# New hand-written instruction orders for all five queues, and four more normalizations on ScalarE, in a fused attention and gated-MLP block

## The chip, the core and the metric

One core of one Trainium2 chip. The metric is the device time of one execution in microseconds (us). The engines that matter: TensorE (PE; its weight loads are shown apart as PEld), VectorE (DVE), ScalarE (ACT), GpSimd (POOL), and the SP queue, which computes nothing and only issues DMAs. ScalarE's queue issues DMAs too.

## The reference

Two branches share one normalized input and are added to it. `x` is 2048 tokens x 512, all in bf16.

```
xn = layernorm(x)
# A: attention over 8 keys, 2 apart, 32 heads of 16
q, k, v = split(xn @ wqkv)
logits[s, w] = q[s] . k[s - 2w] / 4           (w = 0..7, masked where s - 2w < 0)
A = (softmax(logits) weighted sum of v[s - 2w]) @ wo
# B: gated MLP that mixes tokens
z = gelu(xn @ w_in);  z1, z2 = halves of 896
g = w_sp @ layernorm(z2) + b_sp               (w_sp is 2048 x 2048)
B = (z1 * g) @ w_out
out = x + A + B
```

## The kernel before

The kernel is straight-line code without loops on the chip. A small planner in the file (`Plan`) collects tasks. Each has an engine, a name, and the buffers that it reads and writes, from which its dependencies follow. `plan.orders` holds five lists, one for TensorE, ScalarE, VectorE, GpSimd and SP, and each names every task of its queue. A list therefore is the order in which that queue runs; the planner's costs and due times decide nothing more. Every queue is strictly in order: a task that waits holds up all that stand behind it.

The stages, with the names of the tasks and the lines of the profile:

- **Setup and layernorm of x**, for 16 tiles of 128 tokens. `ldx0..15` load rows of x (L588). Per tile, VectorE takes statistics (`bnst`, L650, and `bnag`, L653), GpSimd raises the variance to the power -1/2 (`rstd`, L655), and VectorE normalizes (`norm`, L665). Tiles 0 to 3 are transposed by TensorE (`xTr`, evacuated by `xTe`), tiles 4 to 15 by DMA transposes from SP (`xTd`, L669). GpSimd also makes masks (`mask`, `hm`). Weights come in by `ldq`, `ldk`, `ldw_in1`, `ldwv`, `ldwout`, `ldwo` and others.
- **Q and K**, for four groups j of 512 tokens and four channel groups c: `Qj_c`, `Kj_c` (L733), evacuated together by ScalarE as `QKej_c` (L741); `halo` copies the last 16 columns for the next group (L747).
- **Logits**: VectorE multiplies Q by eight shifted K (`prodj_c`, 4096 columns, L757) and adds the four channel groups (`paddj_n`, L762). TensorE sums over the head with `lgj` (L772), ScalarE evacuates (`lge`).
- **z2 and its norm**: `z2_b` (L852), gelu with a sum by ScalarE (`z2g`), sum of squares (`z2s`, L907). Per wave j of four token tiles VectorE forms mean and variance (`zm`, `zq`, `ze`, `zv`), GpSimd the power -1/2 (`zr`, L926), VectorE a bias (`zb`), and then each tile b is normalized by `znb`, either on ScalarE (L933) or on VectorE (L937). `znact` says where, one entry per wave.
- **z1 and V**: `z1_b` (L895) with gelu `z1g` (L901), `Vq` (L717) with `Ve` (L721).
- **Softmax**: `pT` transposes logits by DMA, `sm`, `ssub`, `sexp` (ScalarE), `sz`, `srec`, `sattn`.
- **Gate and output**, eight steps t, each for two of the 16 output tiles, from tile 14 and 15 down to 0 and 1. The spatial product of 2 x 2 blocks is done with seven products instead of eight: `P1_t` to `P7_t` (L1015), which need sums of weights (`S13`, `S2`, `S4`; L974, L978, L980) and of z2 (`T1` to `T4`, L954). SP brings the weights by DMA transposes straight from DRAM, `wt_0` and `wt_1` (L962), into two slots. ScalarE copies partial results (`cA`, `cB`, `cE`, `g11`, `g21`), VectorE makes `g12` (L1057), `g22` (L1061) and the gated `u` (L1039), which SP transposes (`uT`, L1041). For attention VectorE multiplies (`pv`, L1145) and adds (`pva`, L1149; `pvc`, L1153), and SP transposes (`OTdt`, L1157). `outb` is the final product (L1207 for attention, L1211 for the MLP), onto x put into PSUM by `os`; `fin` evacuates, `st` stores. ScalarE's queue issues `ldxrt`, the rows of x for the residual (L1166), and most `st` (L1182).

PSUM banks are handed out in a fixed turn, so a product waits until ScalarE has emptied its bank. The lines that decide where a norm runs, and what waits for what around it:

```
 655  T("pool", lambda g: g.tensor_tensor(Fv("rstd", 1, b), Fv("mv", 1, 2 * b + 1), Fv("mhalf", 1), ALU.pow),
 656    reads=[("mv", b), "mhalf"], writes=[("rstd", b)], est=580, name="rstd%d" % b)
 ...
 665  T("dve", lambda v: v.tensor_scalar(AC(xo, [[1, 512]]), xin, Fv("mv", 1, 2 * b),
 666                                     Fv("rstd", 1, b), ALU.subtract, ALU.mult),
 ...
 932  if cfg["znact"][j]:
 933      T("act", (lambda b: lambda a: a.activation(A("z2", FH, FH * b), A("z2", FH, FH * b), ACTF.Identity,
 934                                                 bias=Fv("nb2", 1, b), scale=Fv("rstd2", 1, b)))(b),
 935        reads=[("nb2", j), ("rstd2", j)], writes=[("z2l", b), ("z2r", b)], est=c_act(FH), name="zn%d" % b)
 936      continue
```

Of the kernel before, what the change touches and what calls it, by code (L numbers as in the profile page):

```python
# [325 lines left out]
def build_kernel(nc, A_x, A_wqkv, A_wo, B_x, B_w_in, B_w_sp, B_b_sp, B_w_out, out, report=False, sched_kw=None,  # L326
# [90 lines left out]
    with ExitStack() as es:  # L417
# [809 lines left out]
        for t in range(NT):  # L1227
# [16 lines left out]
        plan.orders = [  # L1244
            """
                warm xTr0b fill0 xTr0a z2_0_0b z2_0_1b z2_0_0a xTr1a xTr1b z2_0_1a xNr z2_1_0a z2_1_0b z2_1_1a xTr2a
                xTr2b z2_1_1b z2_2_0a z2_2_0b xTr3b xTr3a z2_2_1a z2_2_1b z2_3_0a z2_3_1a z2_3_1b z2_3_0b Q0_0 K0_0
                Q0_1 Q0_2 K0_1 Q0_3 K0_2 K0_3 Q1_0 K1_0 K1_1 Q1_2 Q1_1 K1_2 Q1_3 K1_3 z2_4 z2_5 z2_6 z2_7 K2_0 Q2_0
                Q2_1 Q2_2 K2_1 K2_2 Q2_3 lg0_0 K2_3 z2_8 z2_9 z2_10 z2_11 K3_0 Q3_0 K3_1 K3_2 Q3_2 K3_3 Q3_3 Q3_1
                z2_13 lg1_0 z2_14 z2_12 z1_14 z1_15 z2_15 z1_13 z1_10 z1_12 z1_8 z1_11 lg2_0 z1_7 z1_9 z1_6 z1_2 z1_4  # L1250
                z1_5 z1_1 z1_3 z1_0 V10 V11 lg3_0 V14 V12 V15 V13 V8 V4 V6 V9 V5 V7 V2 V3 V0 V1 P1_0 P5_0 P6_0 P2_0
                bits P3_0 P7_0 P1_1 P5_1 P4_0 P6_1 P2_1 P7_1 P3_1 P1_2 P4_1 P2_2 P6_2 P5_2 P7_2 P3_2 out14_0 P4_2 P1_3
                out15_0 P2_3 P6_3 P5_3 P1_4 P7_3 P3_3 out12_0 P4_3 P5_4 P6_4 out13_0 P2_4 P7_4 P3_4 P1_5 P4_4 out10_0
                P2_5 P5_5 P6_5 out11_0 P7_5 P3_5 P5_6 P4_5 P1_6 out9_0 P6_6 out8_0 P2_6 out6_0 P1_7 P3_6 P7_6 out7_0
                P5_7 P6_7 P4_6 P2_7 P3_7 P7_7 out4_0 out5_0 P4_7 out3_0 out2_0 out0_0 out1_0 out1_1 out1_2
            """.split(),
            """
                actprime ldw_in2a_1 ldw_in2b_1 ldx2 ctr0 xTe0b xTe0a xTe1a xTe1b xNe z2g0_0 xTe2a xTe2b z2g0_1 z2g1_0
                xTe3a xTe3b z2g2_0 z2g2_1 z2g1_1 z2g3_0 z2g3_1 QKe0_0 z2s0 QKe0_1 QKe0_2 QKe0_3 z2s1 QKe1_0 z2s2
# [17 lines left out]
                prod0_2 bnag12 bnag15 bnst14 bnst13 padd0_1 bnag14 bnag13 prod0_3 norm12 padd0_2 norm15 norm13 norm14
                prod1_0 prod1_1 ze0 padd1_0 zm1 prod1_2 zv0 padd1_1 prod1_3 zq1 zb0 padd1_2 ze1 prod2_0 prod2_1 zm2
                padd2_0 zv1 prod2_2 padd2_1 zq2 prod2_3 padd2_2 zb1 zm3 prod3_0 prod3_1 ze3 zq3 padd3_0 smask ze2
                prod3_2 zv2 padd3_1 zv3 prod3_3 padd3_2 S13_0 zn15 zn8 zn12 zn9 T3_0 zn13 zn10 S2_0 zn14 S4_0 T3_3  # L1280
                zn11 T1_0 T1_3 T3_2 T2_0 sm1_3 T3_1 sm2_3 T2_3 sm3_3 T1_1 ssub3 T2_1 T1_2 T4_0 T4_3 T2_2 sz1_3 T4_1
# [72 lines left out]
```

## Time and profile before

| | |
|---|---|
| median of 3 runs | 231.41 us (230.76 to 232.58) |
| the profiled execution | 229.84 us, span of its instructions 228.1 us |
| granted TensorE clock | 1.000 |
| busy: TensorE, VectorE, ScalarE, GpSimd | 221.1, 211.7, 131.1, 30.7 us |
| moved by DMA | 29.96 MB, mean 131 GB/s |

Times in the views are us from the start of the span. A view of a timeline gives start, length, engine, line, operation, output and input, and in square brackets how long the engine sat idle just before and what ended that; neighbours that do the same are merged (x2 and more). TensorE's busy time is modelled: a matmul counts as busy while it is in the pipeline. A queue's name with a q (SPq, ACTq) means its issuing of DMAs.

### The profile page before, as it was taken

What the parts mean: (1) busy time and instruction counts of PE and PEld (TensorE: products, weight loads), DVE (VectorE), ACT (ScalarE), POOL (GpSimd) and SP (SyncE); (2) the same over time, 40 slices, a digit from 0 to 9 for tenths busy, and PEclk for the clock granted to TensorE, in tenths of its full rate; (3) what the DMA queues carried; (4) which work ended last, traced back from release to release, by engine and by line L of the source; (5) the groups of instructions that cost most, each with busy time, mean ns of one, the idle gap of its engine ahead of it and who ended that gap; (6) DMA issues with size and microseconds to landing.
All of it is one profiled execution on the core that took longest, in us unless ns stands there. A gap on an engine that the chain in (4) does not pass through costs nothing.

```text
span 228.1 us, 3127 instructions
## 1 busy us (share of the span) xinstructions
PE 221.1 (97%) x1163; PEld 121.5 (53%) x1176; DVE 211.7 (93%) x259; ACT 131.1 (57%) x237; POOL 30.7 (13%) x35
## 2 busy tenths in 40 slices
PE   8999999999999999999999999999999998999975
PEld 6545554554676775655454545544454543454434
DVE  4799999999999999999999999999999996999920
ACT  4777989879999899874242504028133226033332
POOL 3345455050220090000000000000000000000000
DMA  6998502390000008939988999939498198427742
GB/s 226 278 188 244 113 15 49 77 241 4 0 3 0 0 0 187 223 87 265 231 140 185 185 177 205 159 80 200 95 205 216 37 172 150 86 92 79 182 86 92
DMA packets 77400, 29.96 MB, mean 131 GB/s; under 512 B 68669, under 2 KB 75339, under 8 KB 77259
## 3 DMA queue, kind: packets, MB, share of 16 engines
q1 hardware_dynamic: 74250, 25.08, 54.6%
q10 hardware_dynamic: 3136, 4.69, 6.8%
q8 instruction: 9, 0.15, 0.3%
q14 instruction: 5, 0.04, 0.1%
HBM read 9.05 MB, written 2.10 MB: 49 GB/s over the span
## 4 chain that ended last, share of the span: by engine, by line
PE 73%; DVE 13%; DMA 9%; issue 3%; ACT 1%; POOL 1%; SPq 0%; DVEq 0%
PE ps L1015 27%; PE ps L733 12%; PE ps L895 11%; PE ps L852 8%; PE ps L717 6%; PE ps L1211 5%; DMA arena<-in_B_w_sp_dram 4%; DVE arena L1149 3%; DVE arena L1145 3%; PE ps L1207 3%; DMA arena<-in_A_wqkv_dram 2%; DMA arena<-arena 1%; DMA arena<-in_A_x_dram 1%; DVE arena L974 1%; PE ps L772 1%
## 5 line engine op out<-in xcount | busy, mean ns | idle before, releaser
L1015 PE MATMUL ps<-arena 128*128 128x448 f16 (+1 forms) x448 | 87.2, 353 | 1.0 <-DVE arena L980 0.9
L1015 PEld LDWEIGHTS ps<-arena 128*128 128x128 f16 (+1 forms) x448 | 43.5, 98 | 43.1 <-DVE arena L980 1.3
L1030 ACT ACTIVATE ps<-ps 128x448 f32<-128x448 f32 x16 | 8.5, 530 | 49.9 <-DVE arena L1057 26.2
L757 DVE TENSOR_TENSOR arena<-arena 128x4096 bf16<-128x4096 bf16 x16 | 36.4, 2287 | 0.2
L1145 DVE TENSOR_TENSOR arena<-arena 128x4096 bf16<-128x4096 bf16 x16 | 36.1, 2278 | 0.0
L733 PE MATMUL ps<-arena 128*128 128x512 bf16 x124 | 28.0, 379 | 0.6 <-DMA arena<-in_A_wqkv_dram 0.4
L1149 DVE TENSOR_TENSOR arena<-arena 128x4096 bf16<-128x4096 bf16 (+1 forms) x16 | 28.0, 1749 | 0.0
L762 DVE TENSOR_TENSOR arena<-arena 128x4096 bf16<-128x4096 bf16 x12 | 27.4, 2287 | 0.1
L1211 PE MATMUL ps<-arena 128*128 128x512 bf16 (+2 forms) x125 | 27.1, 355 | 0.1
L895 PE MATMUL ps<-arena 128*128 128x448 bf16 x128 | 24.8, 353 | 0.0
L733 PEld LDWEIGHTS ps<-arena 128*128 128x128 bf16 x128 | 14.3, 113 | 13.9 <-DMA arena<-in_A_wqkv_dram 0.9
L895 PEld LDWEIGHTS ps<-arena 128*128 128x128 bf16 x128 | 18.4, 145 | 6.2 <-ACT arena L907 0.4
L852 PE MATMUL ps<-arena 128*128 128x448 bf16 x96 | 19.0, 353 | 0.0
L741 ACT ACTIVATE arena<-ps 128x1024 bf16<-128x1024 f32 x16 | 16.0, 1019 | 4.8 <-PE ps L733 4.8
L1211 PEld LDWEIGHTS ps<-arena 128*128 128x128 bf16 x126 | 11.9, 98 | 12.4
L1220 ACT ACTIVATE arena<-ps 128x512 bf16<-128x512 f32 (+2 forms) x17 | 9.4, 561 | 14.0 <-PE ps L1211 13.9
L655 POOL TENSOR_TENSOR fpool<-fpool 128x1 f32<-128x1 f32 x16 | 15.0, 945 | 17.3 <-DVE fpool L653 13.3
L1207 PE MATMUL ps<-arena 128*128 128x512 bf16 (+2 forms) x66 | 15.5, 353 | 1.9 <-DMA arena<-arena 1.5
L1033 ACT ACTIVATE arena<-ps,fpool 128x448 bf16<-128x448 f32 x16 | 10.1, 633 | 12.2 <-PE ps L1015 11.3
L926 POOL TENSOR_TENSOR fpool<-fpool 128x4 f32<-128x4 f32 x4 | 11.5, 2888 | 36.1 <-DVE fpool L924 36.1
L901 ACT ACTIVATE arena<-ps 128x896 bf16<-128x896 f32 x16 | 14.4, 916 | 1.9 <-PE ps L895 1.9
L907 ACT ACTIVATE arena<-arena 128x896 bf16<-128x896 bf16 x16 | 15.2, 948 | 0.0
(85 smaller groups left out, 241.0 us busy)
## 6 DMA issues: line engine op xcount, KB each, us to landing
arena<-in_A_x_dram ACTq DMA_DIRECT2D x8, 256.0 KB, 3.6
arena<-in_A_x_dram SPq DMA_DIRECT2D x15, 128.0 KB, 3.6
out_dram<-arena ACTq DMA_DIRECT2D x7, 256.0 KB, 2.5
arena<-arena SPq DMA_DIRECT2D x1, 1568.0 KB, 8.6
arena<-in_A_wqkv_dram SPq DMA_DIRECT2D x3, 512.0 KB, 4.6
arena<-in_B_w_in_dram SPq DMA_DIRECT2D x1, 896.0 KB, 5.1
arena<-in_B_w_out_dram SPq DMA_DIRECT2D x1, 896.0 KB, 6.2
arena<-arena SPq DMA_TRANSPOSE x40, 3.3
```

What stands on the lines that cost most here:

```text
L733: last = t.matmul(bank(k + which), AC(off["wqk"] + 1024 * dc + col0, [[4, 128]]), AC(off["xnT"] + dc * S + 512 * j, [[1, 512]]), start=(dc ...
L741: T("act", lambda a: a.activation(AC(qo, [[ko - qo, 2], [1, 512]]), ps[:, 512 * k: 512 * k + 1024].rearrange("p (t n) -> p t n", t=2), ACT ...
L757: T("dve", lambda v: v.tensor_tensor(pbv, qb, kb, ALU.mult), reads=[("QT", c, j), ("KT", c, j), ("KTpad", c, j)], writes=[("pb", s_)], est ...
L762: T("dve", lambda v: v.tensor_tensor(A("pb", 4096, 4096 * a), A("pb", 4096, 4096 * a), A("pb", 4096, 4096 * b), ALU.add), reads=[("pb", b) ...
L852: last = t.matmul(ps[:, 512 * (k + hf): 512 * (k + hf) + HF], AC(off["xnT"] + dc * S + 128 * b, [[1, 128]]), AC(off["w_in2"] + FH * dc + H ...
L895: lastm = t.matmul(ps[:, 512 * (k + hf): 512 * (k + hf) + HF], AC(off["xnT"] + dc * S + b, [[NTOK, 128]]), AC(off["w_in1"] + FH * dc + HF ...
L907: T("act", lambda a: a.activation(A("sqj", FH), A("z2", FH, FH * b), ACTF.Square, accum_out=Fv("s2", 1, b)), reads=[("z2h", b, 0), ("z2h", ...
L1015: last = t_.matmul(pb_(k_), st(k), mv(k), start=(start and k == 0), stop=(k == 7), skip_group_check=True)
L1145: T("dve", (lambda iv, tv, av: lambda v: v.tensor_tensor(tv, iv, av, ALU.mult))(iv, tv, av), reads=[("attn", q // 4)] + [("V", i_) for i_ ...
L1149: T("dve", (lambda n: lambda v: v.tensor_tensor(AC(off["Vs"], [[4096, 2], [1, n]]), AC(off["Vs"], [[4096, 2], [1, n]]), AC(off["Vs"] + n, ...
L1207: t_.matmul(po, AC(off["OT"] + 1024 * (t % 3) + 512 * r_ + 128 * cc, [[1, 128]]), AC(off["wo"] + 512 * cc + c0, [[1, n]]), start=False, st ...
L1211: last = t_.matmul(po, AC(off["z1"] + FH * tb + 128 * fc, [[1, 128]]), AC(off["w_out"] + 512 * fc + c0, [[1, n]]), start=False, stop=(fc = ...
```

## The change

One setting, and all five lists. With `znact` at 1 for the third wave, `zn8` to `zn11` (token tiles 8 to 11) run on ScalarE in place of VectorE. No other task is added, removed or altered; the lists hold the same names in another order. The diff, cut to the parts of the lists that are spoken of:

```diff
-    znact=(1, 1, 0, 0),
+    znact=(1, 1, 1, 0),
...
 TensorE
-                xTr2b z2_1_1b z2_2_0a z2_2_0b xTr3b xTr3a z2_2_1a z2_2_1b z2_3_0a z2_3_1a z2_3_1b z2_3_0b Q0_0 K0_0
-                Q0_1 Q0_2 K0_1 Q0_3 K0_2 K0_3 Q1_0 K1_0 K1_1 Q1_2 Q1_1 K1_2 Q1_3 K1_3 z2_4 z2_5 z2_6 z2_7 K2_0 Q2_0
+                xTr2b z2_1_1b z2_2_0a z2_2_0b xTr3a xTr3b z2_2_1a z2_2_1b z2_3_0a z2_3_1a z2_3_1b z2_3_0b K0_0 K0_3
+                Q0_0 K0_1 Q0_1 Q0_2 K0_2 Q0_3 Q1_0 K1_0 Q1_1 K1_1 K1_2 Q1_2 K1_3 Q1_3 z2_4 z2_5 z2_6 z2_7 K2_0 K2_1
...
-                P5_7 P6_7 P4_6 P2_7 P3_7 P7_7 out4_0 out5_0 P4_7 out3_0 out2_0 out0_0 out1_0 out1_1 out1_2
+                out6_0 P1_7 out4_0 P6_7 P5_7 out5_0 P7_7 P2_7 P3_7 P4_7 out2_0 out3_0 out0_0 out1_1 out1_0 out1_2
...
 ScalarE
-                halo0_1 z2s7 QKe2_1 QKe2_2 QKe2_3 halo1_2 lge0 z2g8 z2g9 z2s8 z2g10 z2g11 halo1_3 QKe3_0 halo2_2
-                halo2_0 z2s9 QKe3_2 halo1_1 z2s10 QKe3_3 zn3 QKe3_1 halo2_1 z2g13 lge1 z2g14 z2g12 z2s11 z1g14 z1g15
+                z2s6 QKe2_1 z2s7 QKe2_0 QKe2_2 z2g8 z2s8 halo1_3 QKe2_3 lge0 z2g9 halo2_1 z2g10 z2s9 z2g11 zn0 halo1_2
+                QKe3_0 QKe3_1 z2s10 QKe3_2 zn3 zn2 z2g12 z2g13 z2s11 QKe3_3 z2g15 lge1 z1g14 z2g14 zn7 z2s12 z1g15
...
-                lge2 z1g4 z1g5 zn1 z1g1 zn6 z1g3 z1g0 Ve10 zn0 lge3 Ve14 zn5 Ve12 Ve15 ldxr0 Ve11 Ve13 zn7 Ve8 Ve4 Ve9
+                z1g5 z1g2 zn4 halo2_3 z1g3 lge2 z1g0 zn10 Ve14 z1g1 zn11 Ve12 Ve13 lge3 zn8 Ve15 Ve10 Ve6 Ve8 ldxr0
+                ldxr1 Ve7 zn9 Ve11 Ve9 Ve4 sexp3 Ve2 Ve5 cA_0 Ve3 Ve1 cB_0 Ve0 g11_0 cE_0 sexp2 cA_1 cB_1 os14_0 cE_1
...
-                st1_0_0 ldxr4 g21_4 cB_5 cE_5 os9_0 os8_0 cA_6 fin11_0 ldxr5 os6_0 st2_0_0 cB_6 g21_5 g11_6 cE_6
+                cA_5 os8_0 cB_5 g11_5 fin10_0 ldxr4 g21_4 cE_5 fin11_0 cA_6 os9_0 g21_5 cB_6 fin8_0 os6_0 st2_0_0
+                ldxr5 cE_6 os7_0 fin9_0 fin7_0 st3_0_0 g11_6 ldxr6 os4_0 g21_6 fin6_0 st4_0_0 os5_0 ldxr7 cA_7 cB_7
...
 VectorE
-                zeros steps0 steps1 bnst0 bnag0 ctr1 bnst1 bnag1 norm0 norm1 bnst2 bnag2 bnst3 norm2 bnag3 norm3 bnst7
-                bnag7 bnst6 bnag6 norm7 bnst5 norm6 bnag5 bnst4 norm5 bnag4 bnst9 bnst10 bnag9 norm4 bnag10 zm0_0
-                bnst11 prod0_0 zm0 bnst8 bnag11 zq0 prod0_1 norm10 norm11 bnag8 bnst15 padd0_0 norm9 norm8 bnst12
+                zeros steps0 steps1 bnst0 bnag0 ctr1 bnst1 bnag1 norm0 norm1 bnst2 bnag2 bnst3 norm2 bnag3 norm3 bnst4
+                bnag4 norm4 bnst7 bnag7 bnst5 bnag5 norm7 bnst6 bnag6 norm5 bnst9 zm0_0 norm6 bnag9 zm0 bnst10 bnst8
+                bnag10 prod0_0 bnag8 prod0_1 zq0 norm8 norm10 norm9 bnst11 bnst15 bnag11 padd0_0 norm11 bnst12 bnag15
+                prod0_2 bnst13 bnag12 bnst14 padd0_1 bnag14 bnag13 norm12 prod0_3 ze0 norm15 padd0_2 norm13 norm14
...
-                pva2048_7 pva1024_7 pvc7 u1 zb3 fin1_1 zb2
+                g12_6 pva2048_6 S2_7 pva1024_6 u3 pvc6 u2 pv1 pv0 S4_7 pva2048_7 g22_7 pva1024_7 pvc7 g12_7 u0 zb3 u1
+                fin1_1
...
 GpSimd
-                mhalf ident0 ident1 nident0 nident1 ktpad rstd0 rstd1 rstd2 rstd3 mask0 rstd7 rstd6 rstd5 hm0 rstd4
+                mhalf ident0 ident1 nident0 nident1 ktpad rstd0 rstd1 rstd2 rstd3 rstd4 mask0 hm0 hm1 rstd7 rstd5
...
 SP
-                ldx0 ldx1 ldw_in2a_0 ldw_in2b_0 ldx3 ldx7 ldx6 ldx5 ldx4 ldq ldx9 ldx10 ldk ldx11 ldx8 xTd7 xTd6 xTd5
-                xTd4 ldx15 ldw_in1 ldx12 ldx14 ldx13 xTd11 ldb xTd10 xTd9 xTd8 xTd12 xTd13 xTd15 xTd14 w0_1 w0_0 ldwv
+                ldx0 ldx1 ldw_in2a_0 ldw_in2b_0 ldx3 ldx4 ldx7 ldx5 ldx6 ldk ldq ldx9 ldx8 ldx10 xTd4 xTd7 xTd5 xTd6
+                ldx11 ldx15 ldx13 ldx14 ldx12 xTd10 xTd8 ldb xTd9 xTd11 xTd15 xTd12 xTd13 xTd14 ldwv ldw_in1 w0_0 w0_1
...
-                w3_0 w3_1 w4_0 uT13 uT12 w4_1 OTd1 uT10 w5_0 w5_1 uT11 OTd2 uT8 uT9 w6_0 w6_1 uT6 OTd3 w7_0 OTd4 w7_1
-                uT4 uT7 uT5 OTd5 uT2 uT3 OTd6 uT0 OTd7 uT1 st7_1_0 st7_1_192
+                w3_0 w3_1 uT12 w4_0 uT13 w4_1 OTd1 uT10 w5_0 uT11 OTd2 w5_1 w6_0 uT8 uT9 OTd3 w6_1 w7_0 uT7 w7_1 OTd4
+                uT6 uT4 OTd5 uT5 uT3 OTd6 uT2 OTd7 uT0 uT1 st7_1_192 st7_1_0
```

More of the change, by code (lines that the diff above doesn't have):

```diff
@@ new lines, in build_kernel @@
+                ldxr1 Ve7 zn9 Ve11 Ve9 Ve4 sexp3 Ve2 Ve5 cA_0 Ve3 Ve1 cB_0 Ve0 g11_0 cE_0 sexp2 cA_1 cB_1 os14_0 cE_1
+                g21_0 g11_1 sexp1 cA_2 g21_1 cB_2 cE_2 os12_0 os15_0 fin14_0 g11_2 os13_0 cA_3 g21_2 cB_3 fin15_0
+                g11_3 cE_3 sexp0 cA_4 ldxr3 ldxr2 st0_0_0 g21_3 cB_4 cE_4 fin12_0 g11_4 fin13_0 os10_0 os11_0 st1_0_0
+                cA_5 os8_0 cB_5 g11_5 fin10_0 ldxr4 g21_4 cE_5 fin11_0 cA_6 os9_0 g21_5 cB_6 fin8_0 os6_0 st2_0_0
+                ldxr5 cE_6 os7_0 fin9_0 fin7_0 st3_0_0 g11_6 ldxr6 os4_0 g21_6 fin6_0 st4_0_0 os5_0 ldxr7 cA_7 cB_7
@@ L1277, in build_kernel @@
[L1277 to L1281, printed above, removed]
@@ new lines, in build_kernel @@
+                bnag10 prod0_0 bnag8 prod0_1 zq0 norm8 norm10 norm9 bnst11 bnst15 bnag11 padd0_0 norm11 bnst12 bnag15
+                prod0_2 bnst13 bnag12 bnst14 padd0_1 bnag14 bnag13 norm12 prod0_3 ze0 norm15 padd0_2 norm13 norm14
+                prod1_0 prod1_1 zv0 ze1 padd1_0 zm1 prod1_2 zb0 padd1_1 zq1 prod1_3 zv1 padd1_2 zm2 prod2_0 prod2_1
+                ze2 padd2_0 zb1 zq2 prod2_2 zm3 padd2_1 zv2 prod2_3 smask padd2_2 T3_0 prod3_0 prod3_1 zb2 padd3_0
+                T1_0 prod3_2 ze3 padd3_1 zq3 prod3_3 zv3 padd3_2 T2_0 S13_0 zn12 T4_0 zn13 zn15 zn14 T3_1 S2_0 T1_1
@@ new lines, in build_kernel @@
+                T3_3 S4_0 T2_1 sm1_3 T1_3 sm2_3 T4_1 sm3_3 T3_2 ssub3 T1_2 T2_3 T2_2 T4_3 T4_2 sz1_3 sz2_3 sz3_3 sm1_2
+                srec3 sm2_2 sattn3 sm3_2 pv15 ssub2 pv14 sz1_2 g22_0 sz2_2 S13_1 g12_0 S2_1 sz3_2 S4_1 sm1_1 pva2048_0
+                sm2_1 u14 sm3_1 pva1024_0 ssub1 srec2 g22_1 sz1_1 u15 g12_1 sz2_1 pvc0 sattn2 S13_2 S2_2 sz3_1 u12
+                S4_2 sm1_0 u13 pv12 pv13 g12_2 pva2048_1 sm2_0 g22_2 pva1024_1 u10 S13_3 pvc1 S2_3 sm3_0 pv10 srec1
+                ssub0 S4_3 pv11 g22_3 pva2048_2 S13_4 u11 g12_3 S2_4 sz1_0 pva1024_2 S4_4 pvc2 u8 pv8 pv9 u9 pva2048_3
@@ L1290, in build_kernel @@
+                g22_4 pva1024_3 g12_4 sattn1 u6 S13_5 pvc3 S2_5 sz2_0 pv6 pv7 sz3_0 S4_5 pva2048_4 srec0 pva1024_4
+                g22_5 S13_6 u7 g12_5 sattn0 pvc4 S2_6 pv4 pv5 S4_6 pva2048_5 u5 pva1024_5 u4 pvc5 S13_7 g22_6 pv2 pv3
+                g12_6 pva2048_6 S2_7 pva1024_6 u3 pvc6 u2 pv1 pv0 S4_7 pva2048_7 g22_7 pva1024_7 pvc7 g12_7 u0 zb3 u1
+                fin1_1
             """.split(),
             """
-                mhalf ident0 ident1 nident0 nident1 ktpad rstd0 rstd1 rstd2 rstd3 mask0 rstd7 rstd6 rstd5 hm0 rstd4
@@ L1293, in build_kernel @@
-                hm1 hm2 rstd10 rstd11 rstd9 rstd8 mask1 rstd15 rstd12 rstd13 rstd14 zr0 zr1 zr2 zr3
+                mhalf ident0 ident1 nident0 nident1 ktpad rstd0 rstd1 rstd2 rstd3 rstd4 mask0 hm0 hm1 rstd7 rstd5
+                rstd6 hm2 rstd9 rstd10 rstd8 rstd11 mask1 rstd15 rstd12 rstd13 rstd14 zr0 zr1 zr2 zr3
             """.split(),
             """
-                ldx0 ldx1 ldw_in2a_0 ldw_in2b_0 ldx3 ldx7 ldx6 ldx5 ldx4 ldq ldx9 ldx10 ldk ldx11 ldx8 xTd7 xTd6 xTd5
-                xTd4 ldx15 ldw_in1 ldx12 ldx14 ldx13 xTd11 ldb xTd10 xTd9 xTd8 xTd12 xTd13 xTd15 xTd14 w0_1 w0_0 ldwv
```

35 lines of the change are left out of this document (12 added, 23 removed).

## The prediction

> **What bounds the kernel now.** First the page: TensorE and VectorE are both nearly full, so neither can slip unnoticed.
>
> ```profile
> PE 221.1 (97%) x1163; PEld 121.5 (53%) x1176; DVE 211.7 (93%) x259; ACT 131.1 (57%) x237; POOL 30.7 (13%) x35
> ```
>
> Busy time by stage (columns: stretch and its length, then PE, PEld, DVE, ACT, POOL busy, granted clock, DMA share, GB/s) says where the rest lies. From 48 to 100 us ScalarE has only 52.00 - 48.16 = 3.84 us left; from 186 to 218 both full engines lose something; in the last ten they are half idle.
>
> ```profile
> 48.00:100.00 52.00, 51.90 (x275) 34.05 (x276) 51.83 (x59) 48.16 (x74) 10.79 (x4) 1.00 0.29 66
> 186.00:218.00 32.00, 31.03 (x154) 15.00 (x155) 30.02 (x29) 11.77 (x23) 0.00 (x0) 1.00 0.63 118
> 218.00:228.10 10.10, 6.22 (x50) 3.91 (x48) 0.47 (x3) 2.73 (x8) 0.00 (x0) 1.00 0.41 101
> ```
>
> The chain that ended last (start, length, what) leaves the engines at three DMAs: the K weights, the spatial weights of the last stage (w7_1), and the last transpose of an attention output (OTd7), for which the final output tiles wait.
>
> ```profile
> 8.77 5.18 DMA arena<-in_A_wqkv_dram
> ...
> 181.54 8.99 DMA arena<-in_B_w_sp_dram
> ...
> 217.47 3.26 DMA arena<-arena
> 220.72 0.14 issue
> 220.86 1.02 PE ps L1207 x4
> ```
>
> VectorE's timeline has the one long stall that w7_1 causes, and the short ones at the start, where a norm waits for GpSimd's rstd:
>
> ```profile
> 9.14 0.41 DVE L665 TENSOR_SCALAR arena<-arena,fpool 128x512 bf16<-128x512 bf16 x1 [0.66 <-POOL fpool L655]
> ...
> 190.63 1.23 DVE L974 TENSOR_TENSOR arena<-arena 128x2048 f16<-128x2048 bf16 x1 [1.92 <-DMA arena<-in_B_w_sp_dram]
> ```
>
> GpSimd's timeline shows why the place of an rstd matters. Alone it takes 0.55 us; issued just as VectorE begins a product or sum of 4096 columns (2.29 us) it takes 2.55, ending 0.41 after that instruction (two in the last line):
>
> ```profile
> 10.47 0.55 POOL L655 TENSOR_TENSOR fpool<-fpool 128x1 f32<-128x1 f32 x1 [1.29 <-DVE fpool L653]
> 32.42 5.07 POOL L655 TENSOR_TENSOR fpool<-fpool 128x1 f32<-128x1 f32 x2 [2.45 <-DVE fpool L653]
> ```
>
> **How I count.** Each list is summed with the start-to-start distance of its instructions in this trace, and the lists are joined where one engine needs another. VectorE: prod and padd 2.21, bn_stats 0.63, norm 0.33, zn 0.42, g12/g22 0.59, u 0.53. TensorE tasks: Q, K, V 0.863; z1, z2, P 1.513; lg 0.546; out 2.348. ScalarE's zn is 1.03. The sum is made against the profiled execution: 229.84 us, span 228.1. The median of the runs, 231.41, is 1.57 above it, and I subtract the gain from the median.
>
> **The z2 norm of the third tile.** Four zn leave VectorE: 4 x 0.42 = 1.7 us less there. ScalarE gets 4 x 1.03 = 4.1. Their cover is ScalarE's idle time of 3.84 in that stage, so ScalarE becomes full. The latest, zn9, stands behind lge3: lg3 at 89.0, +0.55 +0.4 to lge3, +0.90, +1.03 (zn8), five Ve at 0.48, +1.13 = 95.4; T3_2, its first reader, is due at 98. So VectorE doesn't wait; without that cover the 1.7 are lost again.
>
> **K before Q.** ldk moves up to the place behind ldx6 (issue 6.74, not 8.77). The load now there landed at 11.30; half a megabyte took 1.45 (9.85 to 11.30) and 1.98 (11.98 to 13.96), so K lands near 11.3, Q by 13.3. TensorE's new start is K0_0 at 12.41, K0_3, Q0_0 at 14.14: no wait for weights, 0.55 saved (Q1_0 starts at 19.31, not 19.86). The transposes it reads: norm6 ends near 15.6, xTd6 issues at 16.0 and lands 3.1 later, just in time.
>
> **The front of VectorE.** norm4 now follows bnag4 directly. bnag4 takes the place of bnag7 (10.20 to 10.39), rstd runs 10.47 to 11.02, norm4 starts at 11.05 instead of 10.31: 0.75 lost. bnag8 now stands directly ahead of prod0_1, and bnag11 directly ahead of padd0_0, so rstd8 and rstd11 begin with them, end 0.41 after them, and norm8 and norm11, which come right after, wait 0.46 and 0.53. (Today rstd11 suffers this too, but norm10 covers it; its wait is 0.12.) norm7 loses 0.1 and norm14 0.2 likewise. Together 2.04, against 0.33 today in that stretch: 1.7 more. If all were hidden the cost is 0; if norm13 and others suffer too, 2.5. I take 1.7.
>
> The Trainium skill, SBUF — State Buffer, section "SBUF: two separate sides", says that GpSimd and a VectorE instruction with two SBUF inputs take a shared port pair as an exclusive lock, and whichever starts first keeps it for its whole length. By that rule rstd8 and rstd11 are blocked, and the trace agrees (2.55 against 0.55). The rule has a second half that no row here shows: rstd13 starts a little ahead of prod0_3 and would hold it up by some 0.3, and the sum would be 229.6.
>
> **TensorE behind it.** Without a wait out0_0 starts at 12.41 + 32 x 0.863 + 28 x 1.513 + 4 x 0.546 + 16 x 0.863 + 56 x 1.513 + 0.19 + 14 x 2.348 = 216.2. Add 0.55 that the four lg cost today beyond their rows. lg1 needs padd1_2: today's end 54.11, 0.22 less work ahead of it, 1.7 lag, 0.1 to pass on: 55.7, while TensorE arrives at 55.3: 0.4. lg3 likewise 0.4. P6_2 needs S2_2: 124.27 - 1.05 + 1.7 = 124.9, TensorE is there at 124.1: 0.75 in starts. So the 0.55 of the weights is given back, and out0_0 could start at 216.2 + 0.55 + 0.8 + 0.75 = 218.3 (today 220.83). I found no later wait: the other sums land 0.5 us or more ahead of their products, and the PSUM banks come free before they are refilled, though some only just (B below).
>
> **SP's queue and the spatial weights.** uT7 now stands ahead of w7_1 and waits for u7 (179.8); behind it wait w7_1, OTd4, uT6. So w7_1 issues at 181.1 to 183.4. Today it landed 9.0 after its issue, beside ldxr5 (issued 181.27) and st2 (182.35); w7_0 landed 4.7 after its own. The new list has ldxr5 and st2 behind cB_6, near 187. Landing at 185.8, or 190.1 if it is slow again: S13_7 is due at 192.1, so the 1.9 of stall goes either way; late next is nothing in that stage. w5_0 likewise issues near 144, with ldxr2 and ldxr3 only after cA_4, near 151. ldw_in1 and ldwv move behind xTd14: issue near 42, 5.05 to land, first z1 near 59. Hidden, cost nothing.
>
> **The end.** pvc7 ends today at 217.44. Take 1.7 (zn) and 1.9 (w7_1) off, and 1.1 for g12_7 and u0, which now come after it; add 1.7 for the front: 214.3. SP issues OTd7, then uT0 at 215.6 (1.23 and more each), then uT1. Of the sixteen uT the undisturbed land 2.9 to 3.1 after issue, the worst 5.7, today's uT0 4.0. I take 3.0, since the stores then in flight end before: 218.6, and 219.8 for uT1. out0_0 starts at 218.7, 2.1 earlier than today; behind it the same 2.2 + 2.6 of TensorE and 2.5 to the end. **Sum: 2.1 us less**, span 226.0, execution 227.7, median 229.3.
>
> **Rivals.** (A) The front costs nothing, because the rstds slip in between. For it: an rstd is ready in 0.55 wherever no long instruction runs. Against: all four setup instructions of GpSimd that met one (rstd11, mask1, rstd13, rstd14) lasted over 2.3. pvc7 then ends at 212.6, out0_0 starts at 217.0: 3.8 gained, 227.6. (B) ScalarE becomes the bound from 47 to 100, and the kernel gets slower. zn0 stands ahead of QKe3_0 in its list and waits for zb0 until 49.1, some 1.3 of idle time, with four more zn to carry: 5.4 in all against 3.84 free. Its queue frees PSUM banks, and by my join two are free only 0.1 ahead of z1_15 and z1_10, so each us that finds no gap goes to TensorE. It decides from 2.1 us on. If none finds a gap, 229.3 + 5.4 = 234.7; if half the free time is usable, 232.8. Against: in the same join ScalarE still waits 1.7 us for TensorE behind z1_15, so most of it fits. The Trainium skill, ScalarE: Activation LUTs, section "Rules for kernel authors", advises VectorE for multiplies and adds; the rows agree on one instruction (508 ns against 1128 ns), and by that rule alone this rival is the outcome. (C) The last transposes land late: uT0 after 4.0 to 4.8 us as today. Then out0_0 starts at 219.7 to 220.5, gain 0.3 to 1.1, near 230.7. For it: two more transposes and a store stand close by. Against: uT1 behind OTd7 took 3.03. (D) The list doesn't keep the row copies apart and w7_1 is slow again: hidden by S13_7's later place, the forecast stays.
>
> **How the numbers follow.** Forecast with D 0.43, A 0.22, C 0.25, B 0.10. The time is the forecast's, 229.3. The range 227.6 to 232.2 takes in A and C, uT0 at its worst, the front between 0 and 2.5, and the mild part of B. One per cent, about what a measurement can tell from no change, is 2.3 us, below 229.1: A and nearly half of the forecast lie there, 0.43. Above 233.7 lies the worse part of B and what I overlooked: 0.07. Between: 0.50.
>
> **What would show it.** In VectorE's timeline: idle 0.7 before norm4, 0.4 to 0.5 before norm8 and norm11, prod1_0 near 39.7 (today 37.98), no wait for w_sp at the last S13. On TensorE: no wait for A_wqkv, short waits at lg1, lg3 and P6_2. In the chain: OTd7 or uT0 released near 218.6 at the end. Wrong would be: VectorE's idle time under 1 us before 40 (A), ScalarE as TensorE's releaser between 47 and 100 for over 2 us in all (B), or a DMA wait inside the gate stages.

## The result, and the profile after

The changed kernel takes 228.22 us (median of 6 runs, 227.82 to 228.66) against 230.69 for the kernel before in the same measurement (229.69 to 232.58): a ratio of 0.9888, 95% interval 0.9844 to 0.9932. A second measurement of both gave 228.14 against 231.34, ratio 0.9867 (0.9838 to 0.9896). So it is faster by somewhat over 1%.

The profiled execution took 228.66 us with a span of 226.9; the spans of the other five were 226.1 to 226.5. Before, the profiled one (229.84, span 228.1) was among the quickest: later runs of it spread from 229.5 to 232.7. The two profiles therefore show 1.2 us of a gain that is 2.5 us in the medians (3.2 in the second measurement). A TensorE task is said here to start with its first weight load.

Busy time on the page after:

```profile
PE 222.4 (98%) x1176; PEld 121.7 (54%) x1176; DVE 210.3 (93%) x255; ACT 134.2 (59%) x241; POOL 35.5 (16%) x35
```

VectorE has 1.4 us less to do and ScalarE 3.1 more, which is where the four zn went. GpSimd is 4.8 us busier although it computes the same, mostly because six of its rstds meet a long VectorE instruction, where three did before. By stage (columns as before):

```profile
48.00:100.00 52.00, 51.48 (x273) 33.56 (x272) 51.97 (x55) 49.15 (x75) 9.12 (x3) 1.00 0.31 73
186.00:218.00 32.00, 32.00 (x161) 15.59 (x160) 30.39 (x29) 12.17 (x23) 0.00 (x0) 1.00 0.52 128
```

ScalarE still has 2.85 us left from 48 to 100, and from 186 to 218 TensorE now has no idle time at all (before, 0.97). The chain that ended last says the same. Its last step on another engine is the sum S2_2 at 125.13; from there on it is TensorE alone up to the last evacuation, where before it went over w7_1 and OTd7:

```profile
123.96 1.15 DVE arena L974
125.13 0.70 DVE arena L978
125.88 6.23 PE ps L1015 x32
...
220.69 1.51 PE ps L1211 x7
```

VectorE's timeline has the price of it, five new stalls ahead of prod1_0 (in brackets), and the last S13 without one:

```profile
10.84 0.41 DVE L665 TENSOR_SCALAR arena<-arena,fpool 128x512 bf16<-128x512 bf16 x1 [0.67 <-POOL fpool L655]
...
14.81 0.69 DVE L650 BATCH_NORM_STATS2 fpool<-arena 128x6 f32<-128x512 bf16 x1 [0.45 <-DMA arena<-in_A_x_dram]
...
22.27 1.05 DVE L665 TENSOR_SCALAR arena<-arena,fpool 128x512 bf16<-128x512 bf16 x3 [0.44 <-POOL fpool L655]
...
27.23 0.43 DVE L665 TENSOR_SCALAR arena<-arena,fpool 128x512 bf16<-128x512 bf16 x1 [0.44 <-POOL fpool L655]
...
39.75 0.41 DVE L665 TENSOR_SCALAR arena<-arena,fpool 128x512 bf16<-128x512 bf16 x1 [0.19 <-POOL fpool L655]
...
192.53 1.21 DVE L974 TENSOR_TENSOR arena<-arena 128x2048 f16<-128x2048 bf16 x1
```

These are norm4, bnst9, norm8, norm11 and norm14, 2.19 us together; prod1_0 starts at 40.08 (37.98 before). On TensorE the lag ends in this wait, P6_2 for S2_2:

```profile
125.88 2.44 PE L1015 MATMUL ps<-arena 128*128 128x448 f16 x12 [0.74 <-DVE arena L978]
```

P6_2 starts 1.56 later than before. Then nothing more is lost, while the kernel before still loses 1.21 at P3_6 (which needs S4_6, and that stands behind the stalled S13_7 in VectorE's list) and 1.89 at out0_0 (behind OTd7). out0_0 starts at 219.45 instead of 220.83.

### The profile page after: what moved, and what is told of

Its sections match the earlier page's. It is cut to its first block, busy times and chain, and to the rows that moved or that the text cites. A ratio compares the mean times of both kernels' runs of the same rounds, so it can differ in the third digit from the quotient of the medians.

```text
span 226.9 us, 3133 instructions
## 1 busy us (share of the span) xinstructions
PE 222.4 (98%) x1176; PEld 121.7 (54%) x1176; DVE 210.3 (93%) x255; ACT 134.2 (59%) x241; POOL 35.5 (16%) x35
## 4 chain that ended last, share of the span: by engine, by line
PE 44%; DVE 40%; POOL 6%; issue 5%; DMA 4%; ACT 0%; POOLq 0%; DVEq 0%
PE ps L1015 27%; DVE arena L757 13%; PE ps L1211 11%; DVE arena L762 7%; POOL fpool L655 6%; PE ps L1207 6%; DMA arena<-in_A_x_dram 4%; DVE arena L954 4%; DVE fpool L650 2%; DVE arena L1145 2%; DVE arena L974 2%; DVE arena L1149 1%; DVE arena L978 1%; DVE arena L820 1%; DVE arena L839 1%
## 5 line engine op out<-in xcount | busy, mean ns | idle before, releaser
L733 PE MATMUL ps<-arena 128*128 128x512 bf16 x128 | 28.5, 380 | 0.0
L1211 PE MATMUL ps<-arena 128*128 128x512 bf16 (+2 forms) x126 | 27.1, 356 | 0.0
L655 POOL TENSOR_TENSOR fpool<-fpool 128x1 f32<-128x1 f32 x16 | 21.1, 1321 | 15.3 <-DVE fpool L653 14.2
L926 POOL TENSOR_TENSOR fpool<-fpool 128x4 f32<-128x4 f32 x4 | 12.2, 3048 | 38.5 <-DVE fpool L924 33.4
L1207 PE MATMUL ps<-arena 128*128 128x512 bf16 (+2 forms) x72 | 16.8, 356 | 0.0
```

Of the source, the lines that this page charges most:

```text
L733: last = t.matmul(bank(k + which), AC(off["wqk"] + 1024 * dc + col0, [[4, 128]]), AC(off["xnT"] + dc * S + 512 * j, [[1, 512]]), start=(dc ...
L1207: t_.matmul(po, AC(off["OT"] + 1024 * (t % 3) + 512 * r_ + 128 * cc, [[1, 128]]), AC(off["wo"] + 512 * cc + c0, [[1, n]]), start=False, st ...
L1211: last = t_.matmul(po, AC(off["z1"] + FH * tb + 128 * fc, [[1, 128]]), AC(off["w_out"] + 512 * fc + c0, [[1, n]]), start=False, stop=(fc = ...
```

## The experiments

Two columns recur: the ratio to the kernel before, and the span of the profiled execution (226.9 with the change, 228.1 before).

The expectations took their ratios from the profiles. In three runs whose spans came out close to what was expected, the ratio was about half a per cent lower (the zn back on VectorE, the two DMAs moved, the two copies put back); that the profile of before is one of its quick executions fits this.

| run | ratio (95%) | span |
|---|---|---|
| changed, again | 0.9867 (0.9838 to 0.9896) | 226.8 |
| front of before, rest changed | 0.9857 (0.982 to 0.9893) | 225.2 |
| front changed, rest of before | 1.0041 (1.0015 to 1.0066) | 229.5 |
| changed, zn8 to zn11 on VectorE | 0.9954 (0.9923 to 0.9985) | 228.5 |
| before, two DMAs moved | 0.9868 (0.9841 to 0.9896) | 226.3 |
| changed, two DMAs moved back | 0.9853 (0.9816 to 0.9891) | 226.7 |
| changed, all norms mended | 1.0092 (1.0056 to 1.0128) | 231.7 |
| changed, local swaps | 0.9846 (0.9812 to 0.988) | 225.7 |
| front of before with K first, rest changed | 0.9876 (0.9844 to 0.9909) | 226.7 |
| changed, local swaps, row loads moved | 0.9806 (0.9784 to 0.9828) | 224.8 |

**The lists cut in two at 40 us.** My theory was that the change is a loss of about 2 us at the front and a gain of about twice that behind it. First the old front with the new rest (the diff in words):

```diff
-  (each list, to norm14 / K1, Q1 / first spatial weights)  order of the change
+  (the same)                                               order of before
```

> All five lists as changed, but their first 40 us (up to norm14 on VectorE, K1/Q1 on TensorE, the first spatial weights on SP, the rstds on GpSimd, z2g3 on ScalarE) in the order of before. Main theory (the gain of the rest is about twice what is left, because the new front puts VectorE 2.1 us back, and it comes out as TensorE's waits at lg1, lg3 and P6_2): prod1_0 starts near 38.0 instead of 40.08, P6_2 near 124.3 instead of 125.88, no wait over 0.4 at lg1, lg3 and P6_2; out0_0 then near 217.9, span near 225.3, some 0.982 to 0.984 of before. Rival F (the front's lag is made up anyway): span as with the change, 226.9, ratio about 0.989. Rival U (without the lag the last transposes or the rest of the list become the bound): P6_2 early, but a new wait before out0_0, span 226 to 227.

Measured: span 225.2; prod1_0 at 38.09, P6_2 at 124.16, out0_0 at 217.73. VectorE's waits from 8 to 41 us, first with the change, then in this run:

```profile
DVE arena L665 <- POOL fpool L655: 2.4, 5, 0.7
DVE fpool L650 <- DMA arena<-in_A_x_dram: 0.5, 1, 0.5
```

```profile
DVE arena L665 <- POOL fpool L655: 0.7, 1, 0.7
```

The main theory's numbers hold to 0.2 us in this execution, which speaks against F and U. The six runs of this kernel spread by 2.0 us, though (226.9 to 228.9), and by the ratio, which missed the expected 0.982 to 0.984, the front's cost can't be told from nothing: 0.9857 against 0.9867 and 0.9888.

The reverse:

> The reverse: the first 40 us in the changed order, all behind it as before, zn8 to zn11 on VectorE. Main theory: prod1_0 near 40.1; VectorE carries the 2.1 us to OTd4, behind which w7_1 is issued, so the stall at S13_7 does not swallow it: pvc7 near 219.5, span near 230.2, ratio 1.009. Rival F (the lag costs nothing): 228.1, ratio 1.000. Rival W (w7_1 is slow only because ldxr5 and st2 are issued beside it; those stand in ScalarE's list, paced by TensorE, and a w7_1 that is issued later meets them less): w7_1 lands in under 9.0 us and the stall shrinks; span 228 to 229.

Measured: ratio 1.0041, span 229.5: slower than before, so the front costs more than nothing. By the profiles it costs 1.4 and not 2.1, as prod1_0 started at 39.27, only 1.3 late; that goes with weights that landed early in this run (K at 11.85). (By the ratio it is less, 0.4% or some 0.9 us.) The lag of 1.3 went through unchanged: OTd4 and w7_1 were issued 1.29 later, w7_1 took 9.06 again, and the stall stood as it had been:

```profile
DVE arena L974 <- DMA arena<-in_B_w_sp_dram: 2.0, 1, 2.0
```

So rival W is wrong here: ldxr5 also moved by 1.28, since TensorE was late too, and all three met as before.

**The zn back on VectorE** (the second line in words).

```diff
-    znact=(1, 1, 1, 0),        zn10 zn11 zn8 zn9 in ScalarE's list
+    znact=(1, 1, 0, 0),        VectorE: ... zn14 zn8 zn9 zn10 zn11 T3_1 ...
```

> The changed kernel with zn8 to zn11 back on VectorE (behind zn14 in its list), all else as changed. Main theory: VectorE is 1.7 us later from 95 us on, nothing later absorbs it, since it never waits there; P6_2 starts near 127.6 instead of 125.88, out0_0 near 221.1, span near 228.6, ratio to before 1.000 to 1.002. Rival W (the gain is w7_1's alone): within 0.3 us of the change, ratio 0.989 to 0.990. Rival B (four zn less relieve ScalarE, which held TensorE up): P1_0 earlier than 100.26.

Measured: span 228.5, ratio 0.9954, P6_2 at 127.45, out0_0 at 221.02: 1.6 us, near the 1.7 that four zn at 0.42 make. Only the place differs. TensorE meets the lag at P5_0 and then at P6_2:

```profile
PE ps L1015 <- DVE arena L954: 1.3, 1, 1.3
PE ps L1015 <- DVE arena L978: 0.8, 1, 0.8
```

The profile puts P5_0's wait down to L954, but T1_2, which P5_0 needs, had ended at 101.68. P5_0 also needs Ve5 to empty its PSUM bank; Ve5 ended at 103.21, 0.12 ahead of P5_0, and stands in ScalarE's list behind sexp3, which had waited 3.05 us for ssub3 on VectorE. P1_0 starts at 100.14, 0.12 earlier than with the change, as does all of this run from Q1_0 on (19.74 against 19.88): taking four zn off ScalarE gives TensorE nothing. Rivals W and B fall.

**Two DMAs moved in the kernel before.**

```diff
-  os9_0 os8_0 cA_6 fin11_0 ldxr5 os6_0 st2_0_0 cB_6 g21_5 g11_6 cE_6
+  os9_0 os8_0 cA_6 fin11_0 os6_0 cB_6 g21_5 g11_6 ldxr5 st2_0_0 cE_6
```

> The kernel before with one edit: ldxr5 and st2_0_0 issued behind g11_6, near 188.5, instead of at 181.3 and 182.4 beside w7_1. Main theory: w7_1 lands 5 to 6 us after its issue instead of 9.0, the 1.92 us stall at S13_7 goes, pvc7 near 215.5, OTd7 lands near 218.8, out0_0 near 218.9, span near 226.2, ratio 0.991 to 0.992. Rival Z (the stall is from something else, or the zn move is the whole gain): w7_1 lands near 190.5 as before, span 228.1, ratio 1.000.

Measured: ratio 0.9868, span 226.3, with no other edit as good as the whole change. By the spans that is 1.8 us, by the ratio 3.0. DMA issues from 181 to 190 us (size, then us from issue to landing), before and in this run:

```profile
arena<-in_A_x_dram ACTq DMA_DIRECT2D x1, 256.0 KB, 4.6
out_dram<-arena ACTq DMA_DIRECT2D x1, 256.0 KB, 8.0
...
arena<-in_B_w_sp_dram SPq DMA_TRANSPOSE x1, 9.0
```

```profile
arena<-in_A_x_dram ACTq DMA_DIRECT2D x1, 256.0 KB, 3.0
out_dram<-arena ACTq DMA_DIRECT2D x1, 256.0 KB, 3.3
...
arena<-in_B_w_sp_dram SPq DMA_TRANSPOSE x1, 5.2
```

In this pair of runs all three are slow together and quick apart. The stall at S13_7 is gone, and the end is still set by OTd7, 1.8 earlier:

```profile
215.70 3.21 DMA arena<-arena
219.05 1.02 PE ps L1207 x4
```

Its six runs lie within 0.64 us, those of before within 2.2 in the same measurement. That the spread of before comes from this landing fits, but was not tried, and it can't be the only source of spread: the old front with the new rest keeps the copies apart and still spread by 2.0.

**Which of the two copies.** The kernel before with one of them moved behind g11_6, the other left beside w7_1; one execution each.

> The kernel before with ldxr5 alone issued behind g11_6; st2_0_0 stays beside w7_1. If the store is what delays the transpose (it landed 0.2 us before w7_1 in the profile before, 8.0 us after its issue): w7_1 still takes 8 to 9 us and S13_7 waits 1 to 2. If the row load is: w7_1 takes 5 to 6 us, no wait. If both add: about 7 us, a wait under 0.5.

> The kernel before with st2_0_0 alone issued behind g11_6; ldxr5 stays beside w7_1. If the store is what delays the transpose: w7_1 takes 5 to 6 us and S13_7 does not wait. If the row load is (4.6 us from issue to landing in the profile before, elsewhere about 3): 8 to 9 us, a wait of 1 to 2. If both add: about 7 us.

Measured: w7_1 takes 6.2 us with the store alone beside it, 6.5 with the load alone; S13_7 doesn't wait in either, spans 226.6 and 226.5. Neither is the culprit by itself. With 5.2 for none and 9.0 for both, the two together cost 3.8, more than 1.0 and 1.3 added. (One copy alone is hardly outside the spread: in the eight runs whose copies came 4.3 us or more after w7_1, it took 4.8 to 6.5.)

**The two copies put back beside w7_1 in the changed kernel.**

```diff
-  cA_6 os9_0 g21_5 cB_6 fin8_0 os6_0 st2_0_0 ldxr5 cE_6
+  cA_6 st2_0_0 os9_0 ldxr5 g21_5 cB_6 fin8_0 os6_0 cE_6
```

> The changed kernel with st2_0_0 issued behind cA_6 and ldxr5 behind os9_0, so near 181.0 and 182, beside w7_1 (181.5) as in the kernel before. Main theory: w7_1 lands about 9 us after its issue instead of 5.85, near 190.5; S13_7 is due only at 192.5 in this list, so it does not wait: span within 0.4 us of the change, ratio 0.988 to 0.991. Rival W (the copies are what the change repaired): a stall of over 1 us before S13_7, span near 228.5. Rival N (something else made w7_1 slow): it lands near 187.3 all the same.

Measured: span 226.7, ratio 0.9853; w7_1 takes 7.7 instead of 5.85 and lands at 188.94, S13_7 starts at 192.28 without a wait. Slower by about half of what I expected (both copies were quick, 3.5 and 3.6), and hidden. So in the changed kernel S13_7's later place behind pva1024_5, u4 and pvc5, which gives the transpose 11 us, suffices by itself; that the copies kept apart would suffice too is shown only in the kernel before.

**The front mended, first try.** All norms behind an instruction that covers their rstd, all but one ahead of padd0_0 (GpSimd's and SP's lists follow):

```diff
-  bnag10 prod0_0 bnag8 prod0_1 zq0 norm8 norm10 norm9 bnst11 bnst15 bnag11 padd0_0 norm11 ...
+  bnag8 zm0_0 zm0 norm9 norm10 prod0_0 norm8 prod0_1 zq0 bnst11 bnag11 bnst15 norm11 bnag15 bnst13
+  norm15 bnag13 bnst14 norm13 bnag14 bnst12 norm14 bnag12 padd0_0 ...
```

> The changed kernel with the order of its first 17 statistics and norms mended: every norm stands behind a statistics instruction or another norm that covers its rstd, rstd8 to rstd15 except rstd12 are done before the next product begins, ldx9 and ldx10 are issued between ldk and ldq; K stays ahead of Q, and everything from prod1_0 on is as changed. Main theory (the stalls at norm4, bnst9, norm8, norm11 and norm14, 0.67 + 0.45 + 0.44 + 0.44 + 0.19 = 2.19 us, are the front's cost): idle before prod1_0 falls by 1.8 or more, prod1_0 starts near 38.2, the waits at lg1, lg3 and P6_2 go, P6_2 near 124.2 or a little earlier, span 224.7 to 225.3, ratio to before 0.981 to 0.986, like the run with the front of before. Rival S (the front costs because K stands ahead of Q or because of TensorE's order, not because of VectorE): prod1_0 earlier, P6_2 still near 125.9, span 226.9. Rival A (the stalls go, but rstds that meet a product still hold up a later norm): idle over 1 us stays, span about 226.

Measured: 1.0092, slower than before. All rstds but rstd12 took 0.55 to 0.57 us, as intended, but VectorE waited for something that I had left out:

```profile
17.61 0.41 DVE L665 TENSOR_SCALAR arena<-arena,fpool 128x512 bf16<-128x512 bf16 x1 [0.64 <-DMA arena<-arena]
18.65 0.41 DVE L665 TENSOR_SCALAR arena<-arena,fpool 128x512 bf16<-128x512 bf16 x1 [0.62 <-DMA arena<-arena]
...
28.35 0.41 DVE L665 TENSOR_SCALAR arena<-arena,fpool 128x512 bf16<-128x512 bf16 x1 [1.91 <-DMA arena<-arena]
```

A normalized tile lies in one of four buffers, so norm9 waits until xTd5 has landed, norm10 for xTd6, norm15 for xTd11: 3.2 us. With the change, where products stand between these norms, none of the three waits appears. prod1_0 came at 43.17, lg0_0 3.35 later than with the change, and P6_2 was still 3.65 later. Another 1.5 us was lost far behind the norms, where S13_3 waited for a spatial weight.

**The front mended, second try.** Only neighbours swapped:

```diff
 VectorE:  bnag4 bnst7 norm4 ...    zq0 norm10 norm9 norm8 ...    padd0_0 bnst12 norm11 ...
 SP:       ldk ldx9 ldq ldx8 ldx10 ...    xTd10 ldb xTd9 xTd8 xTd11
```

> The changed kernel with only these neighbours swapped: norm4 behind bnst7, norm8 behind norm10 and norm9, norm11 behind bnst12, ldx9 issued ahead of ldq, xTd8 behind xTd9. No norm comes earlier than its four-buffer turn allows, so the waits for transposes of the run with all norms mended (3.2 us) should not appear. Main theory (the stalls behind GpSimd and the late ldx9 are the front's cost): no idle over 0.2 at norm4, norm8 and norm11. 0.44 + 0.44 are gained for certain; of the 0.67 + 0.45 ahead of prod0_0 only what QKe0_0 allows, which needs Q0_0, third in TensorE's list: all of it if the weights land as in the run with the changed front (K 11.85, Q 13.28), 0.2 if as in the profile after (13.11, 14.45). prod1_0 between 38.1 and 39.0 instead of 40.08, P6_2 between 124.2 and 125.0, span between 225.0 and 226.0, ratio to before 0.981 to 0.986. Rival S (TensorE's order is the cost): P6_2 near 125.9, span 226.9. Rival M (as with all norms mended, a new wait for a transpose appears): prod1_0 at 40 or later, span 227 and more.

Measured: ratio 0.9846, span 225.7, prod1_0 at 38.79, P6_2 at 124.58. Main theory, inside its range, though by the ratio alone it can't be told from the changed kernel. In place of S2_2, a spatial weight is now the one that is late, w2_0 at P1_2:

```profile
PE ps L1015 <- DMA arena<-in_B_w_sp_dram: 0.6, 1, 0.6
```

**K ahead of Q by itself**, on the kernel with the old front and the new rest:

```diff
-  SP: ldq ldx9 ldx10 ldk      TensorE: Q0_0 K0_0 Q0_1 Q0_2 K0_1 Q0_3 K0_2 K0_3
+  SP: ldk ldx9 ldx10 ldq      TensorE: K0_0 K0_3 Q0_0 K0_1 Q0_1 Q0_2 K0_2 Q0_3
```

> The kernel with the front of before and all behind it as changed (span 225.2), with one edit more: ldk is issued where ldq was and the other way round, and TensorE takes K0_0 K0_3 Q0_0 K0_1 Q0_1 Q0_2 K0_2 Q0_3. By the prediction's step on K before Q: the weight wait of 0.87 at K0_0 goes, Q1_0 starts near 19.3 instead of 19.91, and as TensorE has hardly a wait later, 0.5 us remain: span 224.7, ratio 0.979 to 0.984. Rival Q (Q0_0 comes third and Q lands last, so QKe0_0 and prod0_0 come later and VectorE passes it on): prod0_0 0.3 to 0.9 later than 16.2, a wait of as much at P6_2, span 225.2 to 225.8. Rival L (the weights land later than in the forecast, K near 12 to 13): a wait at K0_0 in place of the one removed, Q1_0 within 0.2 of 19.9, span 225.2.

Measured: K landed at 11.84, K0_0 started at 12.67 without a wait, but Q landed at 14.76 and Q0_0 waited 0.54; Q1_0 at 19.80 against 19.91. VectorE pays for the third place of Q0_0, prod0_0 at 16.95 against 16.20:

```profile
DVE arena L757 <- ACT arena L741: 0.8, 1, 0.8
```

That is rival Q, for the start. The span (226.7) can't be put down to it, because spatial weights also landed late in this run: w2_0 held up P1_2, and w3_1 held up S13_3:

```profile
DVE arena L974 <- DMA arena<-in_B_w_sp_dram: 1.4, 1, 1.4
```

Where K landed at 11.90 and Q at 13.75 (the next run, with the loads of the local swaps) Q1_0 did start at 19.32. But with the local swaps alone the weights landed a little earlier still (11.69 and 13.58) and Q1_0 started at 19.82, since TensorE itself came to K0_0 only at 12.94 instead of 12.44. What K first is worth thus hangs on when Q lands and on when TensorE arrives, which differs by 0.8 us among the runs that didn't wait for K.

**The row loads moved too.** In the runs where w2_0 was late, the transpose pT2 had taken 7.6 to 7.9 us, and ldxr0 had been issued at the same moment. The local swaps, and:

```diff
-  Ve6 Ve8 ldxr0 ldxr1 Ve7 zn9 Ve11 Ve9 Ve4 sexp3 Ve2 Ve5 cA_0 ... g11_1 sexp1
+  Ve6 Ve8 Ve7 zn9 Ve11 Ve9 Ve4 sexp3 Ve2 Ve5 ldxr0 cA_0 ... g11_1 ldxr1 sexp1
```

> The run with the local swaps and one edit more: ldxr0 is issued behind Ve5 (near 99.5) and ldxr1 behind g11_1 (near 117.6) instead of at 92.1 and 92.5, beside the transpose pT2, which took 7.9 us there and held up pT0, pT1 and every spatial weight of steps 1 and 2; w2_0 landed at 119.96, and TensorE waited 0.88 for it at P1_2. Theory (two row copies beside one transpose make it slow, as with w7_1): pT2 takes 3 to 5 us, w2_0 lands by 118, no wait at P1_2, out0_0 near 217.3 instead of 218.19, span near 224.8, ratio 0.980 to 0.984. Rival V (pT2 is slow from something else, or ldxr0 now slows w1_0 as much): w2_0 still lands near 120, span 225.7. Rival E (TensorE comes earlier, but the last transposes or VectorE take over): P1_2 without a wait, a new wait after it, span 225.2 to 225.7.

Measured: ratio 0.9806, span 224.8. SP's queue for the four pT (start, length), with the local swaps alone and with the loads moved:

```profile
90.84 11.78 SPq L803 DMA_TRANSPOSE arena<-arena  x4
```

```profile
90.35 7.04 SPq L803 DMA_TRANSPOSE arena<-arena  x4
```

pT2 takes 3.15 us, w2_0 lands at 117.18, P1_2 doesn't wait, out0_0 starts at 217.38. The theory holds for the transpose, but the span is not its doing. TensorE, no longer held up at P1_2, waits at P6_2 for S2_2 on VectorE instead, the kind of wait that rival E named:

```profile
PE ps L1015 <- DVE arena L978: 0.2, 1, 0.2
```

VectorE is 0.77 earlier in this execution than with the local swaps alone, but it is so from prod1_0 on (38.02 against 38.79), which lies ahead of the moved loads; from there to S2_2 it takes 85.04 in both, and P6_2 to out0_0 takes 93.6 in both. The medians don't differ either (227.13 and 227.10, in two measurements). So what the moved loads are worth beyond the local swaps is not shown. Swaps and loads together beat both kernels; the interval lies below that of the changed kernel in the same measurement, if only just:

> The changed kernel itself, unaltered, beside the same runs of before: for a narrower interval, and for a second profile of the start. Theory L (the weights landed late by chance in the first profile: K 13.11, Q 14.45, while the runs with the same loads had K near 11.9 and Q 13.3 to 14.0): K0_0 near 12.7 to 12.9 instead of 13.15, Q1_0 0.1 to 0.3 earlier, span 226.1 to 226.6. Rival (they belong to the order): K near 13.1 again, span 226.9. Ratio 0.985 to 0.992.

Measured: K landed at 12.03 and Q at 13.50 this time (13.11 and 14.45 in the first profile), K0_0 started at 12.43. That is theory L for the landings of the weights. Yet the span was 226.8, as the rival had it: VectorE's lag (prod1_0 at 39.93) sets P6_2, with the same gap of 1.18 ahead of it, so the 0.7 us at K0_0 are worth 0.16 at out0_0.

## Why the prediction was right, and where it was not

The gain was forecast as 2.1 us; the profiles show 1.2, the medians 2.5. One step of the sum failed (K before Q), one term was too small (the front), and two waits on TensorE were missing.

That the time (228.22) came so near the forecast 229.3 is partly luck. The sum was made against the profiled execution and came out 0.96 too low there (227.7 forecast, 228.66 measured). Then the prediction put the median 1.57 above the profiled execution, because it lay there before. In the changed kernel it lies 0.44 below. Two errors of opposite sign, 0.96 and 2.01, leave 1.1.

- **The zn.** Right. zn9 ended at 95.78 (95.4 predicted), T3_2 started at 98.36 without a wait; moving them back costs 1.6 us. ScalarE's 4.1 us did fit: it waited 1.1 for zb0, as rival B feared, and had 2.85 us left. So the dearer engine was the cheaper place: a zn costs 1.03 us on ScalarE against 0.42 on VectorE, start to start, but TensorE waits for VectorE. That rival's rule, VectorE for multiplies and adds, is in the Trainium skill, ScalarE: Activation LUTs, section "Rules for kernel authors"; the rows agree with it for one instruction, and it did not decide here.
- **The front.** Right in kind: norm4, norm8, norm11 and norm14 stalled by 0.67, 0.44, 0.44 and 0.19 (0.75, 0.46, 0.53 and 0.2 predicted). Mis-sized by a term that was missing: bnst9 waited 0.45, because ldx9 now stands behind ldk and ldq in SP's queue. I had moved ldk past it and not asked who stands behind. prod1_0 came at 40.08, not 39.7. GpSimd's rows show the mechanism; x2 are rstd10 and rstd8, then rstd13 and rstd14:

```profile
10.25 0.55 POOL L655 TENSOR_TENSOR fpool<-fpool 128x1 f32<-128x1 f32 x1 [1.36 <-DVE fpool L653]
...
17.39 4.77 POOL L655 TENSOR_TENSOR fpool<-fpool 128x1 f32<-128x1 f32 x2 [0.77 <-DVE fpool L653]
...
34.22 5.43 POOL L655 TENSOR_TENSOR fpool<-fpool 128x1 f32<-128x1 f32 x2 [2.38 <-DVE fpool L653]
```

  The Trainium skill, SBUF — State Buffer, section "SBUF: two separate sides", has the blocking: of a GpSimd instruction and a VectorE instruction with two SBUF inputs, the one that starts first keeps a shared port pair for its whole length. The five rstds of this trace that began within a product or sum agree (2.3 to 2.6 us against 0.55). The other half, a GpSimd instruction that starts first, did not show: rstd13 started at 34.22, 0.13 ahead of prod0_3, took 2.85, and prod0_3 took its usual 2.28. With the same lead rstd13 took 0.62 in five other runs, the second profile of the changed kernel among them, and prod0_3 again 2.28. In no run did it hold the product up; it either slips through or is held itself, and then norm14 waits the 0.19.
- **K before Q.** This step failed. It had K landing at 11.3 and 0.55 saved. K landed at 13.11 in the first profile (11.7 to 12.5 in the other runs with K first), and Q1_0 started at 19.88, 0.02 later than before. It took the landing from the load that stood in that place before; why K lands later there was not tried. It also left out that VectorE's prod0_0 needs Q0_0, which comes third, and that TensorE's own arrival at K0_0 varies.
- **TensorE behind it.** lg1, lg3 and P6_2 waited 0.35, 0.31 and 0.80 more than before (0.4, 0.4 and 0.75 predicted). P4_0 (0.43, for g22_0) and z2_13 (0.25, for QKe3_2), each for a PSUM bank, were not foreseen. These two and the 0.57 at Q1_0 make 1.25, less 0.09 for the three waits that came out smaller in sum, about the 1.15 by which out0_0 is later than the 218.3 given for TensorE alone.
- **The spatial weights.** Right: w7_1 issued at 181.48 (181.1), S13_7 at 192.53 (192.1) without a wait. Rival D is harmless, as the run with the copies put back shows for a w7_1 of 7.7. The cause, row copies beside it, is shown by the move of the two DMAs in the kernel before; the edit is worth 1.8 us there by the profiles.
- **The end.** pvc7 ended at 214.60 (214.3 predicted, though its terms add up to 214.4), uT0 landed at 219.03 (218.6). But uT0 did not release out0_0 at 218.7, since TensorE itself got there only at 219.45. Rival C, a uT0 that lands 4 us or more after its issue, did not come (3.1). With TensorE earlier uT0 would be next: in the run with the row loads moved it landed at 217.19, and out0_0 started at 217.38.
- **Rival A**, that the front costs nothing, is wrong for this kernel: the stalls are there, and the new front by itself makes the kernel before slower. The old front with the new rest shows what it would have meant (span 225.2).

So by the profiles the gain went like this: about 1.8 us for w7_1 and 1.6 for the zn, 1.7 given back at the front (226.9 against 225.2). Taken one by one these make 1.7, and the profiles show 1.2. They were measured on different kernels, one execution each, and need not add; that TensorE becomes the limit once the stalls are gone fits the chain, but was not tested as the reason. One of the edits alone, the move of ldxr5 and st2_0_0, gives as much as all lists together.

## What to carry to other kernels

When one list of instructions is replaced by another, price the front and the back apart: a stall that is created early and one that is removed late can be of one size, and neither shows in the total. When a step is moved ahead in a queue, ask what stands behind it there (ldx9), what the first reader of the other half is (prod0_0), and how many buffers the thing has (four for the norms). And look at a slow transfer's neighbours before its place: two row copies issued elsewhere were worth as much as five new lists.

## What the runs showed of the hardware

Row copies of 256 KB issued beside a DMA transpose make it slow, and the moment decides. pT2 took 3.15 us with neither copy near, 3.5 with ldxr0 alone issued 0.5 ahead, 3.6 to 3.9 with ldxr0 alone 1.4 to 1.8 behind it (four runs), 4.3 to 4.7 with ldxr0 0.3 and ldxr1 0.7 behind it (four runs), and 7.6 to 7.9 where ldxr0 was issued within 0.01 us of it and ldxr1 0.4 later (four runs); in these, ldxr1 itself took 7.0 to 7.3 and landed 0.2 ahead of pT2. w7_1 shows the like: 5.2 with neither copy near, 9.0 with the load issued 0.3 ahead and the store 0.8 behind (two runs), but 7.7 with the store 0.7 ahead and the load 0.4 behind. Why, the runs do not say.
